# Attention and mixer kernel on one core: batch 0's front and batch 1's pieces in another order

## Chip, cores and metric

One core of one Trainium2 chip runs the whole program. The metric is the device time of one execution in microseconds, and the time before is the median of three runs. A profile is one further execution, recorded by the hardware profiler; its times below count from the span's start.

The engines are PE (TensorE, matrix products), DVE (VectorE), ACT (ScalarE), POOL (GpSimd) and SP (SyncE, which here only issues DMAs). Each runs its own instructions strictly in the order in which they were issued to it, and a wait holds up everything behind it on that engine.

## What is computed

Linear attention with a position weight, then a two-layer token mix and a two-layer channel mix, for 8 batches, 8 heads, 576 positions and 64 values in a head:

```python
def phi(x, c, s):
    r = np.maximum(x, 0.0)
    return np.concatenate([r * c, r * s], axis=-1)
q_p = phi(q, cos_w, sin_w)
k_p = phi(k, cos_w, sin_w)
kv = np.einsum('bhsf,bhsd->bhfd', k_p, v)
z = np.sum(k_p, axis=2)
num = np.einsum('bhsf,bhfd->bhsd', q_p, kv)
den = np.einsum('bhsf,bhf->bhs', q_p, z)[..., None] + 1e-06
x = (num / den)            # then heads side by side: (8, 576, 512)
h = np.maximum(xt @ w_tok1, 0.0) @ w_tok2      # xt: x with positions last; d_tok 256
u = x + h.transpose(0, 2, 1)
h2 = np.maximum(u @ w_ch1, 0.0) @ w_ch2        # d_ch 1536
out = u + h2
```

## The kernel before

The 576 positions of a batch are 4 chunks of 128 (ci 0 to 3, R = 4) and a tail of 64. Two batches share a tail tile of 128 rows: the even one has rows 0 to 63, the odd one 64 to 127. NSC = 5 counts the tail as a chunk, and ORDER = (0, 1, 2, R, 3) is the order of the numerators.

A batch passes through these steps, each a method of `Front` or `Channel`:

- `feature` (L246): cosine (j = 0) or sine (j = 1) half of phi for q or k of one chunk, on DVE as one tensor_scalar (L263) or on ACT as a Relu with a scale (L261). `k_side` and `q_side` do both halves of a chunk; a True in a plan puts the sine half on ACT.
- `q_trans` (L335): transposes of q's features on PE, copied to `qpT` by ACT (L344). From batch 2 on, a DMA transpose on SP does it (L350).
- `values` (L266): v cast into `v_aug`, whose extra column of ones and zero rows are set once at the start.
- `ksum`, `ksum_out`, `dens`, `dens_out` (batch 0 only): sums of k's features (PE, L285), copied to `ks_sb` by ACT (L293), denominators on PE (L302), epsilon and reciprocal on DVE (L306, L307).
- `kv` (L309) and `kv_out` (L328): kv on PE into `kv_ps`, copied to `kv_sb`; half 0 (heads 0 to 3) by ACT, half 1 by DVE (L331). In batch 0 the two halves are separate tiles and separate calls.
- `num` (L353): numerators on PE (L359), divided on DVE into `x_sb` (L369). The two buffers of pool ps_at are shared by kv_ps, num_ps and others; pool ps_mm has four.
- `tok1` (L382) and `tok2` (L406): the token mix on PE, with the sums u on DVE (L409). For batch 0 the transposed u is made directly by PE (L425, L433), since its first channel step waits for it; its tok2 steps follow later, between channel steps.
- `Channel`: `c_main` or `c_block` (L543, L553) makes one of twelve blocks of u @ w_ch1, and ACT writes `h1T` (L547). `o_step` (L576) multiplies two blocks at a time by w_ch2, and DVE adds u (L581).

The order is written out by hand. `first_front` (L633) issues all of batch 0's front, with `busy` matmuls on zeros between the steps of PE. After it, the step list of one batch's channel (12 c steps, slots 0 to 11, then the o steps, from slot O = 12) is walked, and behind each step the work that `pieces` (L461) has planned for that slot: the front of the next batch. An entry (8, V, 2, pool) is thus: after channel step 8, cast chunk 2 of v on POOL.

Loads of q, k and v are issued by SP, apart from the high heads of batch 0's q, which ACT issues. SP, like POOL, issues in order, and each issue also waits for the landing of the DMA eight before it. Weights go through POOL, which casts them to bf16 on the way: w_ch1 in four loads, the first behind `k_done` (landing of k's high heads), and w_ch2 in three, issued in the slots of `pieces` by `load_w_ch2`. Batch 1's loads stand behind w_ch1's second load, batch 2's behind a load of w_ch2. `cast_tok1` and `permute_tok2` (L206 to L212) cast the token weights, on ACT.

Of the kernel before, what the change touches and what calls it, by code (L numbers as in the profile page):

```python
# [16 lines left out]
def kernel(  # L17
# [15 lines left out]
    nc = tc.nc  # L33
# [71 lines left out]
    load_main(qt0, q, 0, HH, H, nc.scalar)  # L105
    load_tail(qtt0, q, 0)
    load_main(kt0, k, 0, 0, HH)
    k_done = load_main(kt0, k, 0, HH, H)
    load_tail(ktt0, k, 0)
    load_main(vt0, v, 0, 0, HH)  # L110
    load_tail(vtt0, v, 0)
    load_main(vt0, v, 0, HH, H)
# [42 lines left out]
    v_augs, x_tails = [], []  # L155
    for i in range(2):
        va = const.tile([P, NSC, H, DP], BF16, name=f"v_aug{i}")
        nc.vector.memset(va[:, 0:R, :, D:D1], 1.0)
        nc.vector.memset(va[half(1 - i), R, :, :], 0.0)
        nc.vector.memset(va[half(i), R, :, D:D1], 1.0)  # L160
        v_augs.append(va)
        xt = const.tile([P, Dm], BF16, name=f"x_tail{i}")
        nc.vector.memset(xt[half(1 - i), :], 0.0)
        x_tails.append(xt)
# [15 lines left out]
    for t in (tail0.kp, tail0.qp):  # L180
        nc.gpsimd.memset(t[half(1)], 0.0)
# [12 lines left out]
    def load_w_ch2(third):  # L194
        ki = third * NCH // 3
        w_ch2_done.append(nc.gpsimd.dma_start(
            out=w_ch2[:, ki:ki + 4, :],
            in_=moe_w_ch2[ki * P:(ki + 4) * P, :].rearrange("(n t) d -> t n d", t=P)))
# [10 lines left out]
    def permute_tok2(ki):  # L209
        nc.scalar.copy(w_tok2[:, ki, 0:SM].rearrange("t (r p) -> t r p", r=R),  # L210
                       w_tok2n[:, ki, 0:SM].rearrange("t (p r) -> t r p", r=R))
        nc.scalar.copy(w_tok2[:, ki, SM:].rearrange("t (g s) -> t g s", g=2),  # L212
                       w_tok2n[:, ki, None, SM:S].to_broadcast([P, 2, ST]))


    class Front:
# [584 lines left out]
```

## Time and profile before

| | |
|---|---|
| three runs | 270.34, 270.86, 271.11 us; median 270.86 |
| profiled execution | 269.59 us, of which the span is 267.8 |
| PE busy, 0 to 18.9 us | 15.93 of 18.90 us |
| PE busy, 18.9 to 58.7 us | 39.80 of 39.80 us |
| PE busy, 58.7 to 67.6 us | 8.63 of 8.90 us |
| PE busy, 67.6 us to the end | 196.61 of 200.20 us |
| TensorE clock granted | 0.9 or more in all 40 slices |

PE's busy time includes the `busy` matmuls and the pipelined ends of others, so a busy PE isn't one at its peak, but a stretch with no gap in the chain can only become shorter by less PE work. In views of the timeline, a line is start, length (of a group from first start to last end), engine, line, operation, output and inputs, and in brackets the idle time before it with what ended it.

### The profile page before, as it was taken

How to read it: one execution, taken by the hardware profiler on the slowest of the kernel's cores; microseconds unless marked ns; L12 is line 12 of the kernel's file. 1: busy time of each engine (PE TensorE's matmuls, PEld its weight loads, DVE VectorE, ACT ScalarE, POOL GpSimd, SP SyncE). 2: the span in 40 equal slices, each digit the busy share in tenths (PEclk: the TensorE clock that was granted, in tenths of full speed). 3: DMA queues.
4: the chain of work that ended last, by engine and by line, in shares of the span. 5: the costliest groups of instructions: out<-in, count | busy, mean ns of one | idle time of the engine just before them, and what ended most of it. 6: DMA issues, size and time to landing. Idle time of an engine off the chain costs nothing.

```text
span 267.8 us, 5125 instructions
## 1 busy us (share of the span) xinstructions
PE 261.0 (97%) x2050; PEld 139.5 (52%) x2050; DVE 164.6 (61%) x376; ACT 129.6 (48%) x228; POOL 13.5 (5%) x24
## 2 busy tenths in 40 slices
PE   7989999999999999999999999999999999999994
PEld 2665466455644455446644455446644455445543
DVE  5965798784465846876565846876565846820022
ACT  4982975428606362546515362537515362526400
POOL 6440230000000000000000000000000000000000
PEclk9999999999999999999999999999999999999999
DMA  7999999999994999479864999289974580270032
GB/s 219 355 264 275 341 160 255 314 205 344 182 344 127 282 178 330 131 194 277 221 219 118 294 217 348 64 178 243 238 252 118 157 120 0 58 198 2 2 110 86
DMA packets 91815, 53.68 MB, mean 200 GB/s; under 512 B 59408, under 2 KB 86928, under 8 KB 91792
## 3 DMA queue, kind: packets, MB, share of 16 engines
q1 hardware_dynamic: 88432, 49.62, 69.5%
q0 software_dynamic: 2832, 3.21, 7.4%
q10 hardware_dynamic: 528, 0.52, 0.6%
q8 instruction: 16, 0.26, 0.4%
q14 instruction: 7, 0.06, 0.1%
HBM read 35.85 MB, written 9.44 MB: 169 GB/s over the span
## 4 chain that ended last, share of the span: by engine, by line
PE 92%; DVE 3%; ACT 2%; DMA 2%; issue 0%; DVEq 0%; ACTq 0%
PE o_ps L576 35%; PE c_ps L543 29%; PE u_ps L406 6%; PE b_ps L382 6%; PE num_ps L359 4%; PE ct_ps L563 4%; PE kv_ps L320 3%; DMA qt<-in_q_dram 2%; DVE qp L263 1%; PE idle_ps L204 1%; PE qT_ps L340 1%; ACT v_aug L274 1%; PE c_ps L553 1%; ACT h1T L547 1%; PE t_ps L433 1%; PE d_ps L302 0%
## 5 line engine op out<-in xcount | busy, mean ns | idle before, releaser
L576 PE MATMUL o_ps<-w_ch,h1T 128*128 128x512 bf16 (+1 forms) x396 | 94.1, 372 | 0.0
L543 PE MATMUL c_ps<-uT,w_ch 128*128 128x512 bf16 (+2 forms) x384 | 92.2, 372 | 0.1
L547 ACT ACTIVATE h1T<-c_ps 128x512 bf16<-128x512 f32 x93 | 55.4, 598 | 59.9 <-PE c_ps L543 59.6
L576 PEld LDWEIGHTS <-h1T 128*128 128x128 bf16 x396 | 37.3, 98 | 39.5 <-issue 0.2
L543 PEld LDWEIGHTS <-w_ch 128*128 128x128 bf16 x384 | 33.5, 97 | 29.6 <-DMA uT<-u_bf 0.3
L581 DVE TENSOR_TENSOR o_sb<-o_ps,u_sb 128x512 f32<-128x512 f32 (+1 forms) x33 | 22.2, 674 | 29.5 <-PE o_ps L576 27.5
L409 DVE TENSOR_TENSOR u_sb<-u_ps,x_sb 128x512 f32<-128x512 f32 x32 | 21.7, 688 | 6.1 <-PE u_ps L406 5.6
L413 ACT CAST u_bf<-u_sb 128x512 bf16<-128x512 f32 x28 | 17.2, 618 | 16.7 <-DVE u_sb L409 16.7
L406 PE MATMUL u_ps<-B,w_tok 128*128 128x512 bf16 x80 | 22.6, 379 | 0.0
L387 ACT ACTIVATE B<-b_ps 128x512 bf16<-128x512 f32 x8 | 4.8, 597 | 35.3 <-PE b_ps L382 35.3
L369 DVE TENSOR_TENSOR x_sb<-num_ps,den 128x512 bf16<-128x512 f32 x28 | 19.4, 691 | 1.0
L563 PEld LDWEIGHTS <-w_ch 128*128 128x128 bf16 x192 | 14.0, 98 | 9.2
L382 PE MATMUL b_ps<-x_sb,w_tok 128*128 128x512 bf16 x64 | 17.9, 379 | 0.0
L563 PE MATMUL ct_ps<-uT_tail,w_ch 128*128 128x128 bf16 x192 | 17.2, 219 | 0.0
L263 DVE TENSOR_SCALAR kp<-kt,cos_t 128x512 bf16<-128x512 f32 x32 | 15.1, 478 | 3.0 <-DMA kt<-in_k_dram 3.0
L274 ACT CAST v_aug<-vt 128x512 bf16<-128x512 f32 (+1 forms) x30 | 16.7, 585 | 0.1
L263 DVE TENSOR_SCALAR qp<-qt,cos_t 128x512 bf16<-128x512 f32 (+1 forms) x35 | 15.9, 453 | 0.9 <-DMA qt<-in_q_dram 0.9
L263 DVE TENSOR_SCALAR qp<-qt,sin_t 128x512 bf16<-128x512 f32 (+1 forms) x35 | 15.9, 453 | 0.0
L331 DVE CAST kv_sb<-kv_ps 128x260 bf16<-128x260 f32 x8 | 3.5, 433 | 18.1 <-ACT kv_sb L331 18.1
L581 DVE TENSOR_TENSOR o_sb<-o_ps,u_tail 128x512 f32<-128x512 f32 x4 | 2.8, 691 | 19.0 <-PE o_ps L576 19.0
L359 PEld LDWEIGHTS <-qpT 128*128 128x128 bf16 x256 | 11.5, 98 | 5.5 <-issue 1.3
L359 PE MATMUL num_ps<-kv_sb,qpT 128*128 128x65 bf16 x256 | 13.0, 193 | 0.9 <-DVE x_sb L369 0.5
(93 smaller groups left out, 232.5 us busy)
## 6 DMA issues: line engine op xcount, KB each, us to landing
out_dram<-o_sb SPq DMA_DIRECT2D x31, 256.0 KB, 3.0
kt<-in_k_dram SPq DMA_DIRECT2D x7, 1024.0 KB, 6.8
vt<-in_v_dram SPq DMA_DIRECT2D x7, 1024.0 KB, 6.3
qt<-in_q_dram SPq DMA_DIRECT2D x7, 1024.0 KB, 8.8
w_ch<-in_moe_w_ch_dram POOLq DMA_DIRECT2D x4, 384.0 KB, 8.1
w_ch<-in_moe_w_ch_dram POOLq DMA_DIRECT2D x3, 512.0 KB, 7.7
out_dram<-o_sb SPq DMA_DIRECT2D x10, 128.0 KB, 2.3
qtt<-in_q_dram SPq DMA_DIRECT2D x8, 128.0 KB, 6.5
```

The lines of the kernel that those rows point to most:

```text
L263: nc.vector.tensor_scalar(o_ap, i_ap, scalar1=w, scalar2=0.0, op0=ALU.mult, op1=ALU.max)
L274: nc.scalar.copy(dst, src)
L359: nc.tensor.matmul(num_ps[:, g, j * DP:j * DP + D1], self.qT_of(ci, h), self.kv_sb[g][:, j, 0:D1], start=True, stop=True)
L369: nc.vector.tensor_mul(self.x_of(ci)[rows].rearrange("p (g j d) -> p g j d", g=2, j=HH), nv[:, :, :, 0:D], den.to_broadcast([rows.stop - r ...
L382: nc.tensor.matmul(self.b1_ps[mi], w, self.x_of(ci), start=(ci == ORDER[0]), stop=(ci == ORDER[-1]))
L406: nc.tensor.matmul(u_ps, w_tok2[:, ki, ci * P:(ci + 1) * P], self.B1[:, ki, :], start=(ki == 0), stop=(ki == NT - 1))
L409: nc.vector.tensor_add(u, u_ps[rows], self.x_of(ci)[rows])
L543: nc.tensor.matmul(c_ps[:, lo:hi], w_ch1[:, ki, mi * P:(mi + 1) * P], uT[:, lo // P:hi // P, ki, :], start=(ki == 0), stop=(ki == NCC - 1))
L547: nc.scalar.activation(self.h1T[:, mi, :], c_ps, AF.Relu)
L563: nc.tensor.matmul(self.ct_ps[:, mi % R, :], w_ch1[:, ki, mi * P:(mi + 1) * P], self.tail.uT[:, ki, :], start=(mi % R == 0 and ki == 0), s ...
L576: nc.tensor.matmul(o_ps, h, w_ch2[:, ki, cols], start=ki == 0, stop=ki == NCH - 1)
L581: nc.vector.tensor_add(o_sb, o_ps, u)
```

## The change

In batch 0's loads, q's high heads go from ACT's queue to SP's, the k tail ahead of k's high heads, and v's high heads are cut in two quarters. In the front, q's tail is transposed over 64 rows alone (`q_trans_tail_first`, with the other half of `qpT_tail` zeroed once by POOL), the k tail's features come before the chunks', ACT makes the sine half of chunk 1 too, v is cast in three parts split between DVE and ACT, all denominators stand ahead of kv, kv's halves share one tile and are both copied by ACT, and the first numerator is made and divided in two halves. `cast_tok1` follows kv_out, one of two `permute_tok2` goes to POOL, as do the fixed values of batch 1's `v_aug`. The `busy` matmuls fall from 33 to 28, and the narrow one in `num` goes.

In the slots of batch 1, batch 0's tok2 comes first and the k features and casts of v behind it; chunk 0 of q has its sine half on ACT. w_ch2 is loaded as blocks 0 to 2, 2 to 4, 4 to 8 and 8 to 12, and batch 0's first two o chunks alternate every two blocks instead of every four. Batch 2's tails are loaded after its main parts, its tail features come last, and batch 3's k is loaded later, with its v and q.

```diff
@@ -102,14 +102,15 @@
     load_main(qt0, q, 0, 0, HH)
-    load_main(qt0, q, 0, HH, H, nc.scalar)
+    load_main(qt0, q, 0, HH, H)
     load_tail(qtt0, q, 0)
     load_main(kt0, k, 0, 0, HH)
+    load_tail(ktt0, k, 0)
     k_done = load_main(kt0, k, 0, HH, H)
-    load_tail(ktt0, k, 0)
     load_main(vt0, v, 0, 0, HH)
     load_tail(vtt0, v, 0)
-    load_main(vt0, v, 0, HH, H)
+    load_main(vt0, v, 0, HH, HH + HH // 2)
+    load_main(vt0, v, 0, HH + HH // 2, H)
@@ -152,16 +153,17 @@
-    v_augs, x_tails = [], []
-    for i in range(2):
...
-        x_tails.append(xt)
+    v_augs = [const.tile([P, NSC, H, DP], BF16, name=f"v_aug{i}") for i in range(2)]
+    x_tails = [const.tile([P, Dm], BF16, name=f"x_tail{i}") for i in range(2)]
+    def fill_fixed(i, eng):
+        va = v_augs[i]
+        eng.memset(va[:, 0:R, :, D:D1], 1.0)
+        eng.memset(va[half(1 - i), R, :, :], 0.0)
+        eng.memset(va[half(i), R, :, D:D1], 1.0)
+        eng.memset(x_tails[i][half(1 - i), :], 0.0)
+    fill_fixed(0, nc.vector)
@@ -177,8 +179,8 @@
     tail0 = Tail(0)
-    for t in (tail0.kp, tail0.qp):
-        nc.gpsimd.memset(t[half(1)], 0.0)
+    nc.gpsimd.memset(tail0.kp[half(1)], 0.0)
+    nc.gpsimd.memset(tail0.qpT[:, :, half(1)], 0.0)
     for g in range(2):
@@ -191,11 +193,10 @@
     w_ch2_done = []
-    def load_w_ch2(third):
-        ki = third * NCH // 3
+    def load_w_ch2(k0, k1):
         w_ch2_done.append(nc.gpsimd.dma_start(
-            out=w_ch2[:, ki:ki + 4, :],
-            in_=moe_w_ch2[ki * P:(ki + 4) * P, :].rearrange("(n t) d -> t n d", t=P)))
+            out=w_ch2[:, k0:k1, :],
+            in_=moe_w_ch2[k0 * P:k1 * P, :].rearrange("(n t) d -> t n d", t=P)))
@@ -206,11 +207,11 @@
-    def permute_tok2(ki):
-        nc.scalar.copy(w_tok2[:, ki, 0:SM].rearrange("t (r p) -> t r p", r=R),
-                       w_tok2n[:, ki, 0:SM].rearrange("t (p r) -> t r p", r=R))
-        nc.scalar.copy(w_tok2[:, ki, SM:].rearrange("t (g s) -> t g s", g=2),
-                       w_tok2n[:, ki, None, SM:S].to_broadcast([P, 2, ST]))
+    def permute_tok2(ki, copy):
+        copy(w_tok2[:, ki, 0:SM].rearrange("t (r p) -> t r p", r=R),
+             w_tok2n[:, ki, 0:SM].rearrange("t (p r) -> t r p", r=R))
+        copy(w_tok2[:, ki, SM:].rearrange("t (g s) -> t g s", g=2),
+             w_tok2n[:, ki, None, SM:S].to_broadcast([P, 2, ST]))
@@ -308,13 +309,8 @@
             if ci == 0 and not hasattr(self, "kv_ps"):
-                self.kv_ps = {}
-                if halves == (0, 1):
-                    both = ps_at.tile([P, 2, 512], F32, name="kv_ps", tag="at")
-                    self.kv_ps = {g: both[:, g, :] for g in range(2)}
-            if ci == 0 and halves != (0, 1):
-                for g in halves:
-                    self.kv_ps[g] = ps_at.tile([P, 2, 512], F32, name="kv_ps", tag="at")[:, 0, :]
+                both = ps_at.tile([P, 2, 512], F32, name="kv_ps", tag="at")
+                self.kv_ps = {g: both[:, g, :] for g in range(2)}
             for g in halves:
@@ -325,9 +321,9 @@
-        def kv_out(self, halves=(0, 1)):
+        def kv_out(self, halves=(0, 1), on_act=(0,)):
             for g in halves:
-                copy = nc.vector.tensor_copy if g else nc.scalar.copy
+                copy = nc.scalar.copy if g in on_act else nc.vector.tensor_copy
                 copy(self.kv_sb[g][:, :, 0:D1],
@@ -345,30 +341,42 @@
+        def q_trans_tail_first(self):
+            qT_ps = ps_mm.tile([P, H, ST], BF16, name="qT_ps", tag="mm")
+            for h in range(H):
+                nc.tensor.transpose(qT_ps[:, h, :],
+                                    self.tail.qp[half(0), h, :, :].rearrange("p a b -> p (a b)"),
+                                    ident[half(0), half(0)])
+            nc.scalar.copy(self.tail.qpT[:, :, half(0)], qT_ps)
...
-        def num(self, ci, fill=0, dens=False):
-            num_ps = ps_at.tile([P, 2, 512], F32, name="num_ps", tag="at")
-            if fill:
-                busy(num_ps[:, 0, HH * DP:512], 1)
-            for h in range(H):
+        def num(self, ci, dens=False, halves=(0, 1)):
+            if halves[0] == 0:
+                self.num_ps = ps_at.tile([P, 2, 512], F32, name="num_ps", tag="at")
+            num_ps = self.num_ps
+            for h in range(halves[0] * HH, (halves[-1] + 1) * HH):
                 g, j = divmod(h, HH)
...
             nv = num_ps[rows, :, 0:HH * DP].rearrange("p g (j d) -> p g j d", d=DP)
+            x = self.x_of(ci)[rows].rearrange("p (g j d) -> p g j d", g=2, j=HH)
             if dens:
                 den = self.d_sb[rows, ci * H:(ci + 1) * H, :].rearrange("p (g j) o -> p g j o", g=2)
+                if len(halves) == 1:
+                    g = slice(halves[0], halves[0] + 1)
+                    nv, x, den = nv[:, g], x[:, g], den[:, g]
             else:
...
                 nc.vector.reciprocal(den, den)
-            nc.vector.tensor_mul(
-                self.x_of(ci)[rows].rearrange("p (g j d) -> p g j d", g=2, j=HH),
-                nv[:, :, :, 0:D], den.to_broadcast([rows.stop - rows.start, 2, HH, D]))
+            nc.vector.tensor_mul(x, nv[:, :, :, 0:D], den.to_broadcast(
+                [rows.stop - rows.start, len(halves), HH, D]))
@@ -469,12 +477,13 @@
                 u, act, pool = before.tok2, nc.scalar, nc.gpsimd
-                plan = [(4, KS, 0), (4, KS, 1), (5, u, 0, ps_at, False), (5, KS, 2, True),
-                        (6, KS, 3, True), (6, u, 1, ps_at, False), (7, KS, R), (7, V, R, nc.vector), (8, V, 0, act),
-                        (8, V, 2, pool), (8, load_w_ch2, 0), (8, V, 3, pool),
-                        (8, load_w_ch2, 1), (8, load_w_ch2, 2),
-                        (8, u, 2, None, False), (9, V, 1, act), (9, u, 3, None, False),
-                        (9, QS, 0), (10, u, R, None, False)]
+                plan = [(4, u, 0, ps_at, False), (5, u, 1, ps_at, False), (6, u, 2, None, False),
+                        (6, KS, 0), (6, KS, 1), (7, u, 3, None, False), (7, KS, 2, True),
+                        (8, u, R, None, False), (8, KS, 3, True), (9, KS, R),
+                        (9, V, R, nc.vector), (9, V, 0, act),
+                        (10, V, 2, pool), (10, load_w_ch2, 0, 2), (10, V, 3, pool),
+                        (10, load_w_ch2, 2, 4), (10, load_w_ch2, 4, 8),
+                        (10, load_w_ch2, 8, NCH), (10, V, 1, act), (11, QS, 0, True)]
                 plan += [(11, KV, ci) for ci in range(NSC)]
@@ -488,6 +497,9 @@
                              (1, KS, 3), (1, QS, 2), (2, QS, 3))
+                elif late:
+                    sides = ((-4, KS, 0), (-3, KS, 1), (0, KS, 2), (1, KS, 3), (1, QS, 0),
+                             (2, QS, 1), (3, QS, 2), (4, QS, 3), (5, KS, R), (6, QS, R))
                 else:
@@ -613,9 +625,9 @@
-                for lo in range(0, NCH, 4):
+                for lo in range(0, NCH, 2):
                     for ci in (0, 1):
-                        o_range(ci, lo, lo + 4)
+                        o_range(ci, lo, lo + 2)
                 rest = (2, 3)
@@ -647,43 +659,45 @@
         f.q_side(R)
-        f.q_trans(R, pool=ps_at)
-        busy(idle_ps, 2)
+        f.q_trans_tail_first()
+        busy(idle_ps, 1)
+        f.k_side(R)
         for ci in range(R):
             f.feature("k", ci, 0)
-            f.feature("k", ci, 1, on_act=(ci > 1))
-            busy(idle_ps, 2)
+            f.feature("k", ci, 1, on_act=(ci > 0))
+            busy(idle_ps, 1)
             f.ksum(ci)
-        f.k_side(R)
-        busy(idle_ps, 2)
         f.ksum(R)
+        f.ksum_out()
         busy(idle_ps, 1)
         for ci in range(R):
-            if ci == 2:
-                f.ksum_out()
-            f.values(ci, nc.scalar, lo_heads)
-        cast_tok1(0)
+            f.values(ci, nc.vector if ci < 2 else nc.scalar, lo_heads)
         f.values(R, nc.vector)
         for ci in range(R):
-            f.values(ci, nc.vector, hi_heads)
-        for ci in (0, 1, 2):
+            f.values(ci, nc.vector if ci < 2 else nc.scalar, (HH, HH + HH // 2))
+        for ci in range(R):
+            f.values(ci, nc.vector, (HH + HH // 2, H))
+        for ci in range(NSC):
             f.dens(ci)
+        f.dens_out(0, NSC * H)
+        busy(idle_ps, 1)
         for ci in range(NSC):
...
         f.kv_out((0,))
-        for ci in (R, 3):
-            f.dens(ci)
-        f.dens_out(0, NSC * H)
+        busy(idle_ps, 1)
         for ci in range(NSC):
             f.kv(ci, (1,))
-        f.kv_out((1,))
-        cast_tok1(1)
-        for ki in range(NT):
-            permute_tok2(ki)
+        f.kv_out((1,), on_act=(1,))
+        for mi in range(NT):
+            cast_tok1(mi)
+        permute_tok2(0, nc.scalar.copy)
+        permute_tok2(1, nc.gpsimd.tensor_copy)
+        fill_fixed(1, nc.gpsimd)
         f.new_uT()
...
-        f.num(ORDER[0], fill=1, dens=True)
+        f.num(ORDER[0], dens=True, halves=(0,))
+        f.num(ORDER[0], dens=True, halves=(1,))
         f.num(ORDER[1], dens=True)
@@ -708,7 +722,7 @@
-    def load_batch(b, which="kvq", behind=None, eng=nc.sync):
+    def load_batch(b, which="kvq", behind=None, main=True, tails=True):
         if b not in io_tiles:
@@ -718,13 +732,14 @@
             dst, tail_dst, src = {"k": (kt, ktt, k), "v": (vt, vtt, v), "q": (qt, qtt, q)}[n]
-            done.append(load_main(dst, src, b, eng=eng))
+            if main:
+                done.append(load_main(dst, src, b))
             if behind is not None and len(done) == 1:
                 after(done[0], behind)
-            if b % 2 == 0:
-                load_tail(tail_dst, src, b, eng)
-            if b % 2 == 0 or b == 1:
-                load_tail(tail_dst, src, b | 1, eng)
+            if tails and b % 2 == 0:
+                load_tail(tail_dst, src, b)
+            if tails and (b % 2 == 0 or b == 1):
+                load_tail(tail_dst, src, b | 1)
         return done
@@ -753,12 +768,15 @@
             if b == 0 and i == NCH:
-                load_batch(2, "kq", behind=w_ch2_done[1])
+                load_batch(2, "kq", behind=w_ch2_done[2], tails=False)
             if b == 0 and i == NCH + 13:
-                load_batch(2, "v")
-            if 0 < b < B - 2 and i == NSC:
+                load_batch(2, "v", tails=False)
+                load_batch(2, "kqv", main=False)
+            if b == 1 and i == 9:
+                load_batch(3, "kvq")
+            if 1 < b < B - 2 and i == NSC:
                 load_batch(b + 2, "vq")
-            if b < B - 3 and i == NCH + (18 if b == 0 else 12):
+            if 0 < b < B - 3 and i == NCH + 12:
                 load_batch(b + 3, "k")
...
                 following = next_front(b + 2)
```

More of the change, by code (lines that the diff above doesn't have):

```diff
@@ L152 @@
     nc.gpsimd.memset(ones[half(1), 1:2], 0.0)
-    v_augs, x_tails = [], []
-    for i in range(2):
[L157 to L163, printed above, removed]
-        x_tails.append(xt)
+    v_augs = [const.tile([P, NSC, H, DP], BF16, name=f"v_aug{i}") for i in range(2)]
[7 more added lines that the diff above has]
+    fill_fixed(0, nc.vector)
     class Tail:
```

## Prediction

> **What bounds the kernel now.** I read the page's busy times and releaser chain first, then the chain of waits for the first 80 us in order of time, then the timeline of the engines.
>
> ```profile
> span 267.8 us, 5125 instructions
> PE 261.0 (97%) x2050; PEld 139.5 (52%) x2050; DVE 164.6 (61%) x376; ACT 129.6 (48%) x228; POOL 13.5 (5%) x24
> ...
> PE 92%; DVE 3%; ACT 2%; DMA 2%; issue 0%; DVEq 0%; ACTq 0%
> ```
>
> TensorE (PE) is the bound nearly everywhere: from 18.9 us on the chain is PE work with no gap up to 58.7 us. What can still move is where PE waits: the front before about 19 us, and any new wait that a reordering puts into the gapless part. This is the front's chain (start, length, what):
>
> ```profile
> 14.48 0.18 PE ks_ps L285 x8
> 14.66 0.24 PE idle_ps L204
> ...
> 14.91 0.74 PE d_ps L302 x24
> 15.65 0.63 PE kv_ps L320 x20
> 16.28 0.40 PE d_ps L302 x16
> ...
> 17.34 0.43 DVE kv_sb L331
> ...
> 17.82 0.29 PE num_ps L359 x4
> ...
> 18.14 0.70 DVE x_sb L369
> ...
> 18.88 0.40 PE num_ps L359 x8
> ```
>
> The k sums end, denominators and kv follow, the second half of kv is copied by VectorE (DVE) after the denominators, and the third numerator (18.88) waits for the first x_sb.
>
> **The front, part by part.** All loads of batch 0 now stand on one SP queue, with q's high heads ahead of the q tail and the k tail ahead of k's high heads. The 512 KB of q's low heads need no longer share: the DMA rates by window (176 GB/s in 2 to 3 us, 318 in 3 to 4) have moved them by 4.1 us; with the half microsecond from last packets to landing that is 4.6 instead of 5.68. That frees ScalarE (ACT) after its eight 0.48 us copies of qpT and a tail copy half as wide (1.01 becomes 0.5) by about 10.6 instead of 12.1. But the next thing needed is k. Its halves land at 8.26 and 10.04 (issues at 2.06 and 2.71, 6.2 and 7.3 us to landing) and the k tail at 10.7 (3.26 plus 7.4). The queue was full, so changing two loads' places leaves the sum: k's high heads now land at about 10.7. Work starts 0.10 after a landing (5.68 to 5.78 in the chain): 10.79. ACT now makes three sine halves; the two of before started 0.71 apart and end 0.81 after their start:
>
> ```profile
> 12.03 1.52 ACT L261 ACTIVATE kp<-kt,bias,sin_t 128x512 bf16<-128x512 f32 x2
> ...
> 14.70 0.17 ACT L293 CAST ks_sb<-ks_ps 128x8 bf16<-128x8 f32 x1 [0.54 <-PE ks_ps L285]
> ```
>
> So the last is ready at 10.79 + 2 x 0.71 + 0.81 = 13.02 (DVE's five halves at 0.40 end at 12.9, beside it), its k sum starts at 13.1, the tail's 0.2 later. From the tail's k sum to the first denominator it was 14.32 (its matmul row) to 14.91, 0.59: the denominators start at 13.9, a full 1.0 earlier. Most of this is handed back. All 40 denominators now stand before kv: 16 took 0.40, so 25 ns each, 1.0 together (the 24 before took 0.74, with 0.30 of weight loads held at issue). With a 0.22 filler kv's low half starts at 15.13, and its copy ends 1.19 later as before (15.51 to 16.70): 16.32. The two halves are now in one PSUM tile, and the built program lets kv's high half wait for that copy: 16.36 against 16.53. Its copy, now on ACT (0.38), ends by 17.6 and is covered by the next wait. The first num is cut in two in one tile, and its high half waits until DVE has read the low half: num low 16.95, DVE 0.32 later (17.82 to 18.14) at 17.27, 0.43 for a half (the 128x256 eviction of L581 took 0.424), num high 17.74 (was 17.82), second half on DVE 18.06 to 18.49, third num 18.53 (was 18.88). **Front: -0.35.** Bounds: k's high heads at their old 10.04 give -0.65 (ACT frees at 10.6); if q's low heads still land at 5.68, ACT frees at 11.5 and it is +0.4.
>
> Fillers fall from 33 to 28 and the tail's transposes read half as much; those lie in these waits and are in the sum. cast_tok1 goes behind kv_out on ACT: 17.5 plus two of 0.51 is 18.6, first used after 18.8: nothing. One half of permute_tok2 (1.11 and 0.30 on ACT) goes to POOL at 16.4, when w_tok2 has landed; even at twice ACT's time it is done by 19.5 and is used at about 22.5. v_aug1's memsets follow there, needed at 32. Nothing for both, unless POOL slows DVE's x_sb (PSUM reads; no row shows such a pair).
>
> **Batch 1's pieces.** The same PE work from the first c_ps to kv took 24.46 to 36.98; so c_ps at 24.11, kv at 36.63. The tok2 steps move ahead, the k features and value casts behind. In the timeline (start, length) ACT runs in step with PE:
>
> ```profile
> 32.08 0.60 POOL L276 CAST v_aug<-vt 128x512 bf16<-128x512 f32 x1 [15.94 <-DMA vt<-in_v_dram]
> ...
> 32.43 0.54 DVE L263 TENSOR_SCALAR kp_tail<-ktt,cos_t 64x512 bf16<-64x512 f32 x1
> ...
> 32.89 0.83 DVE L263 TENSOR_SCALAR kp_tail<-ktt,sin_t 64x512 bf16<-64x512 f32 x1
> ...
> 33.64 0.82 DVE L276 CAST v_aug<-vtt 64x512 bf16<-64x512 f32 x1
> ...
> 35.08 0.61 ACT L274 CAST v_aug<-vt 128x512 bf16<-128x512 f32 x1
> ...
> 36.12 1.03 PE L543 MATMUL c_ps<-uT,w_ch 128*128 128x512 bf16 x4
> ...
> 36.98 1.14 PE L320 MATMUL kv_ps<-v_aug,kp 128*128 128x65 bf16 x32
> 37.18 0.60 ACT L547 ACTIVATE h1T<-c_ps 128x512 bf16<-128x512 f32 x1 [0.70 <-PE c_ps L543]
> ```
>
> An h1T starts 1.06 after its c_ps (36.12 to 37.18) and holds ACT 0.50; a value cast holds it 0.52 and ends after 0.61. Before, the last cast of a value stood at 35.08, 1.9 ahead of kv. Now V0 stands behind the tenth c_ps's h1T and V1 behind the eleventh's. These c_ps start at 34.04 and 34.90, so: h1T 35.10, V0 35.60, h1T 36.12, V1 36.62 to 37.23. PE wants it at 36.63 + 0.24 = 36.87 (eight kv matmuls) and gets it at 37.27: +0.40. Queued behind V1 on ACT are the last h1T (37.14) and the sine half of q, now ACT's (37.63 to 38.44): q's first transposes go at 38.52, where PE would be at 37.27 + 0.94 = 38.21: +0.31. **+0.70** together; both are program order on ACT in step with PE, so an earlier PE doesn't heal them. Then o_ps of two tiles alternate and take two of the four ps_mm buffers, and the tail's transposes wait for a qT copy: copies at 39.16 and 40.07 (0.91 apart in the x3 group of L344), 1.02 long, buffer free at 41.12, PE there at 40.95: **+0.17**.
>
> DVE: after the add of the third tok2 it starts k at 32.32. Eight k halves and two of q at 0.40, two adds at 0.60 and the tail cast at 0.34 come first, then q1's sine, 0.48 long: it ends at 38.34. Its transposes stand at 38.96, a margin of 0.6. POOL's two casts now run beside it. In the lines above three DVE instructions from 32.43 to the next at 34.50 took 2.07, where their usual pitches (0.40, 0.40, 0.34) make 1.13: 0.94 lost beside POOL. Once that, less the margin: **+0.3** (between 0 and the +2.2 of the first rival).
>
> The Trainium skill, "SBUF — State Buffer", section "Who interferes with whom", says that DVE copies, casts and tensor_scalars in a two-port mode and a GpSimd instruction shut each other out for a whole instruction. The lost 0.94 agrees. By the rule, every POOL instruction beside these features would be paid, which is the first rival.
>
> At nothing: the w_ch2 loads, cut 2, 2, 4, 4. Their second and third parts landed at 41.9 and 44.9 (34.14 plus 7.7, 34.88 plus 10.0) and are used at about 43.4 and 46.5; if POOL issues them over 1.5 us late, PE waits. Batch 1's loads (k 28.4, v 32.0, q 35.4 from their issues) keep their gate, w_ch1's second load; first uses at 32.3, 32.1 and 37.0 cover half a microsecond of delay. Batch 2's main loads keep their gate too; its tails go behind v, late by six issues of 0.63, needed by DVE at 63 and by kv at 67.6. SP's five qpT transposes stand behind them; before, they landed about a microsecond ahead of use, but batch 3's 1 MB of k was in front then and is behind now.
>
> **Sum:** -0.35 + 0.70 + 0.17 + 0.3 = +0.8. Span 267.8 becomes 268.6, the profiled execution 269.59 becomes 270.4; the median of the three runs, 270.86, lies 1.27 above that execution, so the time to expect is **271.7**.
>
> **Rivals.** (1) *POOL and DVE shut each other out through the whole stretch* (slower). POOL has two casts and four issues of 0.75 in its queue from 32.1, DVE eleven SBUF instructions. For: the 0.94 lost above. Against: while POOL issued w_ch1's loads from 10.3 to 16.1, DVE's k features kept their 0.47. If it loses two to three times 0.94, 1.9 to 2.8, less 0.6, that is 1.3 to 2.2 in place of 0.3: about 273.1. It decides from 0.6 us of DVE delay on. (2) *ACT's stall is not paid* because h1T and casts start closer than read: then -0.35 + 0.17 leaves 270.7. Against: the pitches come from many rows. (3) *The whole 1.0 of the denominators arrives* (faster): k lands as before and the waits for a half tile cost less than the rows say, and stall (2) is away as well: -1.0 + 0.17, 270.0. Against: the built program's two waits. (4) The change does nothing where PE is the bound, and batch 1's loads gate as before: 270.9.
>
> **Chances.** Forecast 0.47 (own range 271.1 to 272.3, half on either side of 0.3%, 271.67); rival 1 0.22; rival 2 0.14; rival 3 0.11; rival 4 0.06. A measurement of this kernel tells about 0.3%, 0.8 us, from no change. Slower: 0.23 + 0.22 = 0.45. Faster: 0.11 of rival 3 and 0.04 of rival 2's lower end: 0.15. Within: 0.40. The range leaves rival 3's end and the worst of rival 1: 270.0 to 273.4.
>
> **What would show it.** The first d_ps near 13.9 and the third num near 18.5; kv of batch 1 waiting for ACT's v_aug and q's first transposes for ACT's qp; kv_sb waits of PE on ACT in the front. If the third num is before 18.0, or PE has no gap at 37 to 39, the sum is wrong; kp of 0.8 us on DVE beside POOL would speak for rival 1.

## The result, and the profile after

The changed kernel takes 274.94 us (median of 273.50, 274.81, 275.06 and 275.58), the kernel before 270.60 in the same comparison: 1.0153 times as long, with an interval of 1.0116 to 1.0190. The prediction had the sign as its likeliest case, but 271.7 us, a range that ends at 273.4, and a sum a fifth of the real one. One execution each of e1, e5, e7 and of the kernel before took 344 to 771 us; the ratios below leave it out, and without it those medians would be 0.02 to 0.23 us lower.

The profiled execution took 274.81 us. From its page, the span, the engines' busy time and the granted clock in 40 slices of 6.8 us:

```profile
span 272.8 us, 5097 instructions
...
PE 261.9 (96%) x2022; PEld 141.1 (52%) x2044; DVE 163.4 (60%) x374; ACT 129.4 (47%) x229; POOL 13.8 (5%) x31
...
PEclk9956999999999999999999999999999999999999
```

The third and fourth slice show 5 and 6: TensorE's clock was at half there. The clock records of the trace put it at 0.5 from 14.45 to 24.69 us, 10.24 us long, and at 1.0 from then on until the last instructions. The busy times by window say what came ahead of it (window, its length, then PE busy and PE's instructions; the eighth number, behind the five engines, is the granted clock):

```profile
10.30:14.90 4.60, 2.15 (x54) 1.70 (x56) 4.22 (x12) 2.72 (x6) 3.06 (x4) 0.95 1.11 341
14.90:18.90 4.00, 3.53 (x77) 3.20 (x75) 1.26 (x7) 1.07 (x4) 0.00 (x0) 0.50 1.11 293
18.90:24.60 5.70, 4.88 (x49) 3.16 (x48) 3.51 (x6) 2.63 (x5) 2.70 (x6) 0.50 1.14 217
```

Before, PE was busy for 4.43 of the 4.60 us in the first of these windows, and the clock was 1.00 in all three:

```profile
10.30:14.90 4.60, 4.43 (x62) 2.73 (x62) 4.54 (x14) 3.91 (x9) 4.58 (x3) 1.00 1.09 382
```

The front's chain after (start, length, what), against the one shown of before, whose first channel step was the line `24.62 2.59 PE c_ps L553 x12`:

```profile
11.55 0.89 DVE kp L264 x2
...
13.97 0.42 PE ks_ps L286 x16
...
14.63 1.21 PE d_ps L303 x40
...
16.28 1.11 PE kv_ps L316 x20
...
17.42 0.39 ACT kv_sb L327
...
17.86 1.26 PE kv_ps L316 x20
...
20.77 0.60 PE num_ps L364 x8
...
28.30 2.59 PE c_ps L565 x12
```

The denominators do start earlier (14.63, before 14.91). But 20 matmuls of kv take 1.11 us where they took 0.63, the second half of kv waits for ACT's copy of the first, the third numerator starts at 20.77 (before 18.88), and the first channel step at 28.30 (before 24.62). That is 3.68 of the 5.0 us by which the span grew. From that c_ps to batch 1's first (61.10, before 56.51) it is another 0.91, and a wait of a numerator of batch 2 for `qpT_tail`, to 78.50, adds 0.37. 3.68 + 0.91 + 0.37 = 4.96.

### The profile page after: what moved, and what is told of

Same layout as the page of the kernel before. It is cut to its first block, busy times and chain, and to the rows that moved or that the text cites. A ratio compares the mean times of both kernels' runs of the same rounds, so it can differ in the third digit from the quotient of the medians.

```text
span 272.8 us, 5097 instructions
## 1 busy us (share of the span) xinstructions
PE 261.9 (96%) x2022; PEld 141.1 (52%) x2044; DVE 163.4 (60%) x374; ACT 129.4 (47%) x229; POOL 13.8 (5%) x31
## 4 chain that ended last, share of the span: by engine, by line
PE 82%; DVE 8%; DMA 4%; ACT 2%; issue 1%; SPq 1%; DVEq 0%; ACTq 0%
PE o_ps L588 33%; PE c_ps L555 24%; PE b_ps L390 7%; PE u_ps L414 6%; PE ct_ps L575 3%; PE kv_ps L316 3%; PE num_ps L364 3%; DMA kt<-in_k_dram 3%; DVE x_sb L378 3%; DVE kp L264 1%; DMA qpT_tail<-qp_tail 1%; ACT v_aug L275 1%; PE c_ps L565 1%; DVE den L376 1%; ACT h1T L559 1%
## 5 line engine op out<-in xcount | busy, mean ns | idle before, releaser
L588 PE MATMUL o_ps<-w_ch,h1T 128*128 128x512 bf16 (+1 forms) x380 | 92.6, 372 | 0.6
L390 PE MATMUL b_ps<-x_sb,w_tok 128*128 128x512 bf16 x63 | 18.8, 398 | 0.2 <-issue 0.2
L275 ACT CAST v_aug<-vt 128x512 bf16<-128x512 f32 (+2 forms) x30 | 16.4, 580 | 0.1
L364 PEld LDWEIGHTS <-qpT 128*128 128x128 bf16 x256 | 12.2, 102 | 5.7 <-issue 0.7
L364 PE MATMUL num_ps<-kv_sb,qpT 128*128 128x65 bf16 x256 | 13.9, 200 | 0.6 <-DVE x_sb L378 0.5
L316 PEld LDWEIGHTS <-kp 128*128 128x128 bf16 x256 | 11.7, 102 | 4.5 <-issue 1.3
```

What stands on the lines that cost most here:

```text
L316: nc.tensor.matmul(self.kv_ps[g][:, j * DP:j * DP + D1], self.k_of(ci)[:, g * HH + j, :, :] .rearrange("p a b -> p (a b)"), self.va[:, ci, ...
L364: nc.tensor.matmul(num_ps[:, g, j * DP:j * DP + D1], self.qT_of(ci, h), self.kv_sb[g][:, j, 0:D1], start=True, stop=True)
L390: nc.tensor.matmul(self.b1_ps[mi], w, self.x_of(ci), start=(ci == ORDER[0]), stop=(ci == ORDER[-1]))
L588: nc.tensor.matmul(o_ps, h, w_ch2[:, ki, cols], start=ki == 0, stop=ki == NCH - 1)
```

## Experiments

The times in a heading are the run's median and that of the kernel before in the same comparison. A "streamed share" is worked out from the trace: the columns of all matmuls that start in a stretch of 3.41 us, at the 0.216 us that 512 columns take at full clock (twice that at half), over 3.41. The half clock lasted 3.41 us or two, three or four times that in every profiled run that had it (e6 the two), so the stretches are laid out from the first record of the full clock on.

### Was it the clock, or the late k?

**e1: fillers back (272.90; before 270.68).**

```diff
         f.q_trans_tail_first()
-        busy(idle_ps, 1)
+        busy(idle_ps, 10)
...
-            busy(idle_ps, 1)
+            busy(idle_ps, 2)
             f.ksum(ci)
```

> The changed kernel with more filler matmuls in the front: ten instead of one behind the query tail's transposes (into the 2.3 us in which TensorE waits for k), two instead of one per k chunk. Theory 1 (the granted clock fell to half because TensorE was too thinly busy from about 10 to 14.5 us, and that half clock is most of the front's +3.7): the clock stays at 1.0 behind 4 us, the first d_ps stays near 14.6, the first c_ps of L565 comes at 24.9 +- 0.4 instead of 28.3, and the time falls from 274.9 to 271.5 (271.0 to 272.0). Theory 2 (k's high heads land late, and the half clock only falls into a wait that is there anyway): first c_ps within 0.5 of 28.3 and the time within 0.4 of 274.9, whatever the clock does.

Ratio 1.0093 (1.0069 to 1.0118). The clock stayed at 1.0, in the chain:

```profile
14.83 1.14 PE d_ps L303 x40
...
16.21 0.62 PE kv_ps L316 x20
...
25.25 2.59 PE c_ps L565 x12
```

The first c_ps comes at 25.25 instead of 28.30: the half clock is worth 3.05 us of the front, though thirteen matmuls more are issued. The time fell by 2.0 only, and that was not expected: 1 us of it comes back in batch 1 (below).

**e3: the old order of the loads, fillers thin (274.60; before 270.68).** q's high heads go on ACT's queue and the k tail behind k's high heads.

> The changed kernel with q's high heads back on ACT's queue and the k tail back behind k's high heads; the fillers stay thin. Theory 1: k's high heads land near 10.0 again, TensorE is as thinly busy as before, the clock still falls to half, only some 0.5 us earlier: 274.3 (273.5 to 275). Theory 2: the late k was the cause, the front is near the predicted one: 271.3 (270.8 to 271.8).

Ratio 1.0144 (1.0113 to 1.0176). k's high heads landed at 9.71 instead of 11.46, the clock still fell for 10.24 us (14.53 to 24.77), and the first c_ps came at 28.16. The late k is not the cause of the half clock.

**e2: the kernel before with seven fillers less (270.46; before 270.68).**

```diff
-        busy(idle_ps, 2)
+        busy(idle_ps, 1)
...
-            busy(idle_ps, 2)
+            busy(idle_ps, 1)
             f.ksum(ci)
         f.k_side(R)
-        busy(idle_ps, 2)
         f.ksum(R)
```

> The kernel before with seven of its filler matmuls taken away in the front (one behind the query tail, one per k chunk, two ahead of the tail's k sum: some 1.5 us of the 4.4 us that TensorE is busy from 10.3 to 14.9 us); nothing else is changed. Theory 1: the clock falls to half here too, and the time rises to 273.5 (272.5 to 274.5); if the clock stays at 1.0 with about 2.9 of 4.6 us busy, the point at which it falls lies between that and the 2.15 of the changed kernel. Theory 2: fillers that lie in waits cost nothing and are worth nothing: 270.6, within 0.3.

Ratio 0.9998 (0.9975 to 1.0022): a miss for theory 1's size. The clock did fall, in nine of the twelve runs by their mean clock and in the profiled one for a single 3.41 us (14.98 to 18.40), but k's sums, no longer paced by fillers, let the denominators start at 14.21 instead of 14.91. In this execution gain and loss nearly cancel: the first c_ps comes at 24.91, before at 24.62. Over the runs less is shown: the three at a mean clock of 1.0 took 269.74 to 270.83 us, the six that lost about one window 270.12 to 270.50, the three that lost about two 270.99 to 271.60. So the gain isn't seen in the three, nor the price of the first window, and the run can't say what the fillers are worth.

**e8: as long at work, but with one column (275.75; before 270.79).** Against e5 below, which has the changed front alone with ten fillers and a clock of 1.0:

```diff
-        busy(idle_ps, 10)
+        busy(idle_ps[:, 0:1], 86)
```

> As e5, but the ten fillers of 512 columns (2.15 us) are replaced by 86 matmuls of one column (25 ns each, 2.15 us): TensorE issues matmuls for just as long but streams 86 columns instead of 5120. If the clock's gate goes by the columns streamed, it falls to half near 14.5 us as in the changed kernel, the first c_ps is beyond 26.5 and the time 3 us over e5 (273.4, 272.5 to 274.5). If it goes by the time in which TensorE is at work at all, the run agrees with e5 within 0.4.

4.7 us over e5, more than the 3 expected: the half clock lasted 13.65 us, four windows, and the first c_ps came at 29.45 (e5: 25.32). In the window in which the 86 matmuls stand, and in the next:

```profile
8.68:12.09 3.41, 3.26 (x103) 2.97 (x103) 2.59 (x8) 3.40 (x7) 1.07 (x2) 1.00 1.12 342
12.09:15.50 3.41, 3.24 (x61) 2.09 (x59) 2.62 (x12) 1.59 (x5) 2.13 (x3) 0.50 1.08 364
```

PE is busy for 3.26 of 3.41 us, and the clock falls all the same, at the end of the window. Its streamed share is 0.22. So PE's busy time, as the profile shows it, does not tell when the clock falls; the streamed columns do here.

**e10: thin fillers, all of batch 1 as before (271.84; before 270.33).** The changed kernel with batch 1's pieces, w_ch2's three loads and the o steps of before.

> e7_front_b2 with the changed kernel's thin fillers (one instead of ten behind the query tail): the changed kernel with batch 1's pieces, w_ch2's loads and the o steps as before. If the costs of the half clock and of the pieces simply add (2.0 from the changed kernel less e1, 2.2 from e1 less e7), this is 274.94 less 2.2: 272.7 (272.3 to 273.1). If the half clock costs its full 3.0 at the first c_ps and, by moving DVE's features 3 us behind POOL's casts, hid a part of the pieces' cost (0.9 in the changed kernel's trace against 1.9 in e1's), this is 270.74 plus 3.0: 273.8 (273.4 to 274.3).

Neither single number: the twelve runs split by their mean clock.

| mean granted clock | about so long at half clock | times, us |
|---|---|---|
| 1.0 | 0 | 269.91, 270.39, 270.55, 270.60 |
| 0.991, 0.994 | 3.4 us | 271.10, 271.75 |
| 0.985 to 0.987 | 6.8 us | 271.94, 272.14, 272.80 |
| 0.979 to 0.981 | 10.2 us | 273.31, 273.47, 273.66 |

The same program thus keeps the clock or loses it. From no to three windows at half clock it is 270.5 to 273.5, the 3.0 that the second branch gave. In the profiled run, at 1.0, the wait for k (1.16 us idle) fell into a window whose share was 0.38 and the next had 0.48; in the changed kernel a window held most of the wait and all of k's sums, with 0.19. PE's busy time again tells nothing: it was 2.25 us in e10's window of 0.38, which kept the clock, and 2.90 in e2's window of 0.24 (from 11.57), which lost it. Over the profiled runs, the windows after which the clock fell had 0.19, 0.22, 0.24 and 0.26 (the changed kernel, e8, e2, e3), and the thinnest after which it stayed had 0.29, 0.36, 0.38 and 0.39 (e7, e5, e10, and e6 in its front). But e6 lost the clock later, from 43.49 us on, after a window of 0.32. Counted by starts that lies above e7's 0.29; if each matmul's columns are spread over its own length, e7's window has 0.35 and e6's stays at 0.32. So of the windows at full clock every one at 0.26 or less was followed by the half clock and none at 0.36 or more; what decides in between is not shown.

The profiled execution also has the front that was predicted. k's high heads landed at 10.72, and by the matmuls' own starts in the timeline the first d_ps comes at 13.92 (predicted 13.9), the third numerator at 18.60 (18.53) and the first c_ps at 24.19 (24.11; before 24.46). The time doesn't show this gain of 0.27: from there to batch 1's first c_ps it takes 0.64 longer than before, 0.31 of it a wait for a load of w_ch2 that landed at 46.29.

Beside the changed pieces a lost window costs less: the changed kernel took 273.50 with about one, 274.81 and 275.06 with three and 275.58 with four, and e1, with none, 272.9. Against the table that is 2.4 more with none, 2.1 with one and 1.5 with three, as it would be if the half clock hid a part of what the pieces cost.

### The front and batch 2's loads without the pieces

**e5: the changed front alone, ten fillers (271.08; before 270.79). e7: the same with batch 2's changed loads and pieces (270.74; before 270.79).**

> The changed front alone: the changed kernel with ten filler matmuls (instead of one) behind the query tail's transposes and still one per k chunk, and with all of batch 1's pieces, w_ch2's three loads, the turns of four o steps, and batch 2's loads and pieces as before. Theory 1 (the half clock was what spoiled the front, the rest of the prediction's front holds): the clock stays at 1.0, k's high heads land near 10.6, the first d_ps comes at 13.9 +- 0.2 and the first c_ps of L565 at 24.3 +- 0.3 (24.62 before), time 270.4 (269.9 to 270.9). If one filler per k chunk is too thin even behind the ten, the clock falls again: first c_ps beyond 26.5 and the time over 272.5. Theory 3 (the waits of one PSUM tile's halves cost more than the 0.65 the prediction gave back): clock 1.0, first d_ps near 13.9, but the first c_ps at 24.8 or later and the time 271.0 to 271.6.

> As e5, but with the changed loads and pieces of batch 2 (its tails on SP behind v, batch 3's loads behind them). The prediction had this at nothing: then it agrees with e5 within 0.3. The theory that SP's transposes of the queries now come too late (in the changed kernel numerators of batch 2 waited for qpT_tail until 78.50) expects +0.4 (+0.2 to +0.7) over e5.

Ratios 1.0010 (0.9990 to 1.0030) and 1.0000 (0.9981 to 1.0020). Both keep the clock. The first d_ps comes at 14.90 and 14.98, not 13.9: k's high heads landed at 11.43 and 11.05, and the ten fillers then hold PE until 13.02 in e5. From the first d_ps to the first c_ps it is 10.42 in e5 and 10.43 in e7 in the chain, and before it was 9.71. By the matmuls' own starts in the timeline, which the prediction's 13.9 and 24.11 are, it is 10.26 in both, 9.55 before and 10.21 in the prediction. So the waits for half a tile hand back 0.71 where the prediction had 0.66, and theory 3's first c_ps and time are met (25.32 and 271.08 in e5), but not for its reason: the price is nearly the predicted one, while the first d_ps isn't early, and so the front gains nothing here. e7's trace shows waits of 0.30 and 0.40 for SP's transposes in batch 2; from batch 1's first c_ps on it is 0.74 longer than e5's, ahead of that 0.51 shorter, and its time is not above e5's.

### The order of batch 1's pieces

**e4: the kernel before with the changed pieces (271.75; before 270.68).**

> The kernel before with the changed order of batch 1's pieces alone (with the loads of w_ch2 in four parts and the o steps of two tiles in turns of two). The prediction's sum for it (+0.70 of ACT, +0.17 of a buffer, +0.3 of DVE): 271.8; the trace of the changed kernel showed +0.9: 271.5. So the theory that the pieces cost something of their own expects 271.3 to 272.0. Rival: that stage was late in the changed kernel only because its loads and weights came a microsecond later behind the longer front, and the pieces alone cost nothing: 270.6, within 0.3.

Ratio 1.0052 (1.0027 to 1.0077): the pieces cost something of their own, in time about as much as the prediction's sum had. The profiled run took 272.95, the longest of the nine (six took 270.93 to 271.84), so what its trace shows need not stand in the median. In it PE idles for 1.51 us in batch 1's stage, and then comes this, in the chain:

```profile
53.89 5.68 DMA uT<-u_bf
59.57 0.05 issue
```

With four loads of w_ch2 the load that batch 2 waits for lands later (43.73, before 41.88). SP issues batch 2's loads from 43.87 on, and u's transposes stand behind them: 1.95 more. The changed kernel doesn't have that, since it moved batch 2's tails behind.

e1 less e7 is what the pieces, with their loads of w_ch2 and turns of o steps, cost at full clock: 272.90 - 270.74 = 2.2 (2.4 by the lower medians). In e1's trace PE idles for 1.87 in batch 1's stage (the sum of start to start less the usual pitch), where e7 has no gap but those that a missing matmul record leaves; in the changed kernel it was 0.93. DVE and POOL in e1, from the timeline:

```profile
33.63 0.83 DVE L264 TENSOR_SCALAR kp<-kt,sin_t 128x512 bf16<-128x512 f32 x1
34.38 0.83 DVE L264 TENSOR_SCALAR kp<-kt,cos_t 128x512 bf16<-128x512 f32 x1
35.13 0.82 DVE L264 TENSOR_SCALAR kp<-kt,sin_t 128x512 bf16<-128x512 f32 x1
...
37.47 0.77 DVE L264 TENSOR_SCALAR kp<-kt,cos_t 128x512 bf16<-128x512 f32 x1
38.27 0.49 DVE L264 TENSOR_SCALAR kp_tail<-ktt,cos_t 64x512 bf16<-64x512 f32 x1
...
33.34 0.84 POOL L277 CAST v_aug<-vt 128x512 bf16<-128x512 f32 x1 [11.27 <-DMA vt<-in_v_dram]
34.13 0.72 POOL L197 DMA_DIRECT2D w_ch<-in_moe_w_ch_dram  x1
34.85 0.82 POOL L277 CAST v_aug<-vt 128x512 bf16<-128x512 f32 x1
35.63 2.36 POOL L197 DMA_DIRECT2D w_ch<-in_moe_w_ch_dram  x3
```

Three features in a row start every 0.75 instead of every 0.40 us, while POOL casts, issues a load and casts again; a later one, at 37.47, takes 0.80 to the next beside an issue alone. POOL's casts go when v lands; DVE's features go 8 us after the first c_ps, behind three adds. In the changed kernel the half clock had moved the features (from 36.28 on) past POOL's casts (33.82 and 35.10). That this is why 1 us less was lost there is argued from two traces; e10's split, above, agrees with it.

**e6: POOL's casts on DVE (280.31; before 270.79). e9: the same, with w_ch2's first load behind v (273.14; before 270.33).**

```diff
-                        (10, V, 2, pool), (10, load_w_ch2, 0, 2), (10, V, 3, pool),
+                        (10, V, 2, nc.vector), (10, load_w_ch2, 0, 2), (10, V, 3, nc.vector),
```

In e9, also:

```diff
+        if len(w_ch2_done) == 1:
+            after(w_ch2_done[0], loads1[1])
```

> e1_after_fill with batch 1's two value casts taken from POOL and given to DVE, behind the tail's cast; all else as in e1 (272.9). Theory A (the prediction's first rival: POOL's casts beside DVE's k features stretch these from 0.40 to 0.75 each, and that is most of what the pieces cost): the features go back to 0.40, DVE pays two casts of 0.34 in their place, the time falls to 272.1 (271.7 to 272.5). Theory B (the forecast's: what the pieces cost is ACT's value casts and q's sine in program order behind h1T): DVE was not the limit, and its two casts more make it 273.2 (272.8 to 273.6).

> As e6 (batch 1's two POOL casts on DVE, fillers as in e1), but w_ch2's first load now waits for batch 1's values to land, as it did behind POOL's first cast; so only the engine of the two casts differs from e1 (272.9). Theory A (POOL's casts beside DVE's k features are most of what the pieces cost): with the casts gone the features keep 0.40 except beside POOL's four load issues, DVE pays 0.76 for its two casts, the time falls to 272.2 (271.7 to 272.6). Theory B (ACT's value casts and q's sine in program order are the cost): no gain, and DVE's two casts add to it: 273.1 (272.8 to 273.7).

e6 says nothing on either theory: POOL's casts had also held back w_ch2's loads, which now went out at 21.2, and v landed at 40.69 instead of 33.21. PE waited for it, and the clock fell for 6.83 us behind that wait:

```profile
41.39 0.42 PE L316 MATMUL kv_ps<-v_aug,kp 128*128 128x65 bf16 x8 [3.00 <-ACT v_aug L275]
```

e9 mends that. Its median lies in Theory B's range, with six runs from 272.26 (the profiled one) to 274.59; what it can show of Theory A is in its trace. POOL only issues loads from 33.00 on, and beside that DVE keeps its pace:

```profile
33.15 0.48 DVE L266 TENSOR_SCALAR kp<-kt,cos_t 128x512 bf16<-128x512 f32 x1
33.54 0.48 DVE L266 TENSOR_SCALAR kp<-kt,sin_t 128x512 bf16<-128x512 f32 x1
33.94 0.48 DVE L266 TENSOR_SCALAR kp<-kt,cos_t 128x512 bf16<-128x512 f32 x1
...
33.00 3.11 POOL L197 DMA_DIRECT2D w_ch<-in_moe_w_ch_dram  x4 [11.24 <-DMA vt<-in_v_dram]
```

Here no feature is stretched by an issue; in the changed kernel two were, to 0.64 and 0.53 (36.67 to 37.31 and 37.70 to 38.23, with POOL issuing from 35.66). So an issue alone stretches a feature now and then, and the three in a row came with the casts. PE's idle time in this stage fell from 1.87 to 1.17, with DVE making two casts more.

**e12: ACT's casts one step earlier (272.88). e13: k's first features back ahead of the adds (272.65); before 270.87, both on e1.**

```diff
-                        (8, u, R, None, False), (8, KS, 3, True), (9, KS, R),
-                        (9, V, R, nc.vector), (9, V, 0, act),
+                        (8, u, R, None, False), (8, KS, 3, True), (8, V, 0, act), (9, KS, R),
+                        (9, V, R, nc.vector), (9, V, 1, act),
...
-                        (10, load_w_ch2, 8, NCH), (10, V, 1, act), (11, QS, 0, True)]
+                        (10, load_w_ch2, 8, NCH), (11, QS, 0, True)]
```

That is e12; e13 is:

```diff
-                plan = [(4, u, 0, ps_at, False), (5, u, 1, ps_at, False), (6, u, 2, None, False),
-                        (6, KS, 0), (6, KS, 1), (7, u, 3, None, False), (7, KS, 2, True),
+                plan = [(4, KS, 0), (4, KS, 1), (4, u, 0, ps_at, False), (5, u, 1, ps_at, False), (6, u, 2, None, False),
+                        (7, u, 3, None, False), (7, KS, 2, True),
```

> e1_after_fill (272.9) with ACT's two value casts of batch 1 each one c step earlier, so that the second no longer stands behind the eleventh h1T. Theory B (the forecast: ACT's program order is what the pieces cost, +0.70): TensorE's wait of 0.39 for the second value cast goes and the time falls by 0.4 to 0.7, to 272.3 (272.1 to 272.5). Theory A (DVE's chain of adds, k features, tail cast and query features sets when the queries' transposes can start, and ACT's wait only lies ahead of that one): the 0.39 goes, the wait for DVE's tail cast grows by as much, the first query transposes still come near 40.2, time 272.9 within 0.3.

> e1_after_fill (272.9) with the k features of batch 1's first two chunks back at the fourth c step, ahead of the adds of u, as before; ACT's and POOL's casts stay as changed. Theory A (DVE's chain, with POOL's casts beside it): four features run at 0.40 in DVE's idle time before 32 us, no longer beside the casts, the waits for DVE (0.58, 0.37, 0.26 in e1) go for the most part and only ACT's 0.39 and 0.3 are left, time 271.8 (271.3 to 272.2). Theory B (ACT): the waits on ACT were all that counts, the time stays at 272.9 within 0.3.

In time e12 is Theory A. PE's timeline in e1, and then in e12:

```profile
38.24 0.89 PE L316 MATMUL kv_ps<-v_aug,kp 128*128 128x65 bf16 x24 [0.23 <-ACT v_aug L275]
39.55 0.40 PE L316 MATMUL kv_ps<-v_aug,kp_tail 128*128 128x65 bf16 x8 [0.42 <-DVE v_aug L277]
```

```profile
39.34 0.40 PE L316 MATMUL kv_ps<-v_aug,kp_tail 128*128 128x65 bf16 x8 [0.62 <-DVE v_aug L277]
```

The wait for ACT is gone and the wait for DVE behind it is 0.2 longer; the queries' first transposes start at 39.96 instead of 40.16, so half of the 0.39 is seen in this execution, and none of it in the median (272.88 against 272.90). In e13 PE's idle time in this stage falls from 1.87 to 0.93, and what is left are waits for ACT (0.39, 0.23) and one of 0.18 ahead of the tail's transposes, until ACT's second copy of a qT_ps has freed a buffer. Its time fell by 0.25 only, within a spread of 271.81 to 273.75; most of the expected 1.1 was not seen, and why is open. In time, then, e12 speaks for Theory A, and e9 and e13 lie in Theory B's ranges. The profiled executions of e9 and e13 (272.26, 272.14) are 0.6 and 0.7 shorter than e1's (272.87), about as their idle times have it, but the medians don't follow. So that DVE's features beside POOL's casts set this stage is read from the traces alone; what makes up the 2.2 in most executions stays open.

### A version that might beat both

**e11: the kernel before, its fillers where PE waits anyway (270.08; before 270.33).** One filler behind q's tail, then 1, 1, 3 and 2 ahead of the k sums, none ahead of the tail's.

> The kernel before with its fillers put where TensorE waits anyway: one behind the query tail, 1, 1, 3 and 2 ahead of the four k sums and none ahead of the tail's (instead of 2, four times 2 and 2). From e2, where k's sums came 0.7 earlier but the clock fell for 3.4 us: the three fillers more than there bring the streamed share of the window from 11.6 to 15.0 us from 0.24 to about 0.43, so the clock stays at 1.0, the first d_ps comes at 14.2 to 14.4 (14.91 before) and the time is 270.1 (269.7 to 270.5). If the clock falls all the same it is 270.7 to 271.3.

Ratio 0.9992 (0.9968 to 1.0015). The clock held, with a share of 0.47 in the window from 11.73 us; the first d_ps came at 14.24 and the first c_ps at 24.02, 0.6 earlier than before. The time agrees with 270.1, but the measurement can't tell it from no change.

## Why the prediction was wrong, step by step

- **"Fillers fall from 33 to 28 [...] those lie in these waits and are in the sum."** This step failed. The fillers did lie in waits, and they weren't free: they kept the clock at 1.0. Without them PE works at half speed from 14.45 to 24.69, 3.05 us at the first c_ps (e1). No rival had it; the row nearest to it is the profile's of before, where the clock stands at 9 in every slice while PE's front is held busy by matmuls on zeros. It also makes the time depend on the run (e10).
- **k at 10.79.** In ten profiled runs with this order of loads k's high heads landed between 10.62 and 11.49: five of them at 10.62 to 10.74, as predicted (10.7), and three at 11.43 to 11.49, the changed kernel's (11.46) among them. 14.63 instead of 13.9 is this; in e10, with 10.72, it is 13.92. The value was right, but the range had no room for how far it varies.
- **"Most of this is handed back."** Right: the waits for kv's copy and for the first numerator's low half stand in the trace where the prediction put them. The price is 0.71 (e5, e7, by either view) where the prediction's 13.9 and 24.11 make 0.66. In e10's profiled execution the whole front came as it was added up.
- **ACT's +0.70 and the buffer's +0.17.** The waits are there, 0.39, 0.23 and 0.18 (e13), 0.40, 0.31 and 0.17 predicted. But in e1, with the clock as the prediction had it, they lie ahead of a later wait for DVE and decide next to nothing (e12).
- **DVE's +0.3.** Mis-sized, and the second thing that failed: at full clock the pieces cost 2.2 in time (e1 less e7) and 1.87 of idle time, within the first rival's 1.3 to 2.2, and the trace has the stretched features that it named; that these are what costs is not confirmed in time (e9 and e13 came out no faster than Theory B had it). In the changed kernel the stage lost only 0.91, near the forecast's +1.17, but with the half clock having moved the features past POOL's casts: luck.
- **Batch 2's loads "at nothing".** In time right (e7). In the traces not quite: from batch 1's first c_ps to the end it takes 211.46 to 211.55 in the six with the old loads (before, e2, e4, e5, e8, e11) and 211.73 to 212.27 in the nine with the changed ones, with `qpT_tail` late by 0.37 in the changed kernel. The pieces' w_ch2 loads at nothing: in e4's trace not, since batch 2's tails still stood ahead of u's transposes there.
- **Rivals 2 and 3.** Their sums leave out DVE's +0.3 as well as ACT's stall, without saying so; nothing above depends on it.

Altogether: 2.0 us of the measured +4.3 is what the clock cost beside the changed pieces (274.94 less e1), 2.2 is the pieces, and the changed front by itself, with fillers, can't be told from 0 (e5 1.0010, e7 1.0000, each give or take 0.002).

## What to carry to other kernels

Before a filler is removed or work in front of a wait is made thinner, count the columns that TensorE streams in each 3.4 us around it, not its busy time; losing the clock cost 0.7 to 1 us per window here, and fillers that end before the wait does cost nothing (e11, against e5's ten, which held up k's sums). When work of two engines is reordered, look where each one's start comes from: here POOL's from a landing and DVE's from PE's progress, so that any shift of the front changes how they collide. And a wait that is taken away shows its worth only if no later one ends behind it (e12).

## What was not expected of the hardware

- The clock went to half although PE was never idle for a whole window: in e8's window for 0.15 us in all, in the changed kernel for 2.35 us at most (10.14 to 12.49), in e6 for 3.00 (38.39 to 41.39). The Trainium skill, "TensorE: Matmul & The Clock Gate", section "HAM oscillation", puts the rule as no idle gaps of PE over about 3.4 us; by that the clock would have stayed at 1.0 in the changed kernel, e2, e3, e6 and e8. The runs decide: a window with a streamed share of 0.26 or less was enough, in e6 one of 0.32. The same page's free-running window of 3413 ns (section "The HAM clock gate") agrees with the half clock's lengths of 3.41, 6.83, 10.24 and 13.65 us and with e10's split.
- Once lost, the clock took one window to come back in e2, two in e6, three in the changed kernel and e3 and four in e8, although PE streamed 0.69 to 0.82 of the half clock's columns in some of the windows that did not bring it back, and 0.79 in the one of e2 that did. What decides the return stays open.
- While POOL casts, issues and casts again, DVE's features start every 0.75 instead of every 0.40 (e1); beside load issues alone one was stretched now and then (to 0.80 in e1, to 0.64 and 0.53 in the changed kernel) or none at all (0.39 in e9).
